# A sketched linear attention feeding an MLP: new order of steps, earlier small loads and table load, attention numerators over four PSUM banks

## The chip, the cores and the metric

The kernel runs on one core of a Trainium2 chip. Its engines each take their instructions in order: TensorE multiplies matrices (in the profile PE, and PEld for the loading of weights), VectorE is DVE, ScalarE is ACT, GpSimd is POOL, and SyncE is SP. SP and ACT also issue DMAs. The metric is the device time of one execution in microseconds (us); lower is better. Engines wait for each other on semaphores.

## The reference

Two parts follow each other. The first is an attention without softmax, for 4 batches, 4 heads, 1088 tokens and 32 values per head. Two sketch matrices S1 and S2 of 8 x 32 turn each query and key into 64 features, the products of 8 values with 8 others:

```python
def phi(x):
    a = np.einsum('rd,bhsd->bhsr', S1, x)
    b = np.einsum('rd,bhsd->bhsr', S2, x)
    return np.einsum('bhsi,bhsj->bhsij', a, b).reshape(*x.shape[:-1], r * r)
q_p, k_p = (phi(q), phi(k))
kv = np.einsum('bhsf,bhsd->bhfd', k_p, v)
z = np.sum(k_p, axis=2)
num = np.einsum('bhsf,bhfd->bhsd', q_p, kv)
den = np.einsum('bhsf,bhf->bhs', q_p, z)[..., None] + 1e-06
return (num / den).astype(np.float32)
```

The second takes the 4352 tokens, each with the 4 heads' 32 values as 128 inputs, through an MLP:

```python
h = x @ w_in                                # 128 -> 2048
g = h * (1.0 / (1.0 + np.exp(-beta * h)))
return (g @ w_out).astype(np.float32)       # 2048 -> 128
```

## The kernel before

**Units.** Each batch's 1088 tokens are laid out as 34 units of 32 tokens and 32 partitions' worth of head values, so that a 32 x 32 block transposition on VectorE (helper `tr`, L161) turns one form into the other. A batch has 9 columns of units in 4 groups (the last group is short).

**Steps and their order.** Nothing is issued as it is written. Every step is registered with `add(engine, name, function, reads, writes)`, and at the end `steps.issue` calls them in the order of the string ORDER (L18), which must respect the reads and writes. So ORDER alone sets the order in which each engine meets its instructions; names in it, such as `kproj1`, `qp2.0.3` or `h4.5`, are the names used below. An element-wise product of any step is the helper `mul` (L152), a copy L156 or L158.

**Set-up.** `fill` and ten `idle` steps give TensorE matmuls of no use to the result (L313). `st` transposes S1 and S2, and `wk`, `wq0`, `wb4` and `wab` lay them out as weights; `s2sel`, `sel`, `rep`, `m4` and `zmask` are selection matrices made from iotas. `beta0` to `beta3` spread beta over the partitions by a matmul of one row (L392), ScalarE copies it out (`betac`), and GpSimd makes `winp` = w_in x beta and `woutp` = w_out / beta in float16 (`w_in`, L407, and `w_out`, L414), so that the activation Silu gives g x beta.

**Keys.** For batch 0, `keys_first` (L491) transposes k in three pieces as its loads arrive, projects it (`kproj0.u`, L509), copies the result to SBUF on ScalarE (`kab`), and forms the 64 features per key on VectorE and GpSimd (`kp`). For batches 1 to 3, `keys` (L537) does the same with block transpositions: `kT`, `kproj` (L546), `kab`, `kp`. In both, `zsum` (`z`, L443) sums features, `wmat` (`W` and its copy `ww`, L460) brings z to the queries' form, `kvsum` (`kv`, L474) makes the features' product with v, and `kvturn` (`kvt`) transposes it. z, W, kv and the later step w all write PSUM bank A2, and each counts as one writer of the whole bank. kv has to stand on all four partition groups: in batch 0 that is a matmul (`km`, then `spread`, L638, and the copy `kvr0`); in batches 1 to 3 it is a DMA to a scratch in DRAM (`scw`, L569) and four DMAs back (`scr`, L575).

**Queries.** The first 8 units of batch 0 go a way of their own (`head`, L590: `abA`, `bS`, `qpA`, `wA`, `numA`, `xA`), so that the MLP can start early. All others go through `queries` (L645): `qproj` (L655) and `w` (L666) on TensorE; `qab`, `qw`, `m`, `den`, `rden`, `an` on VectorE; the 64 features `qp` on VectorE and GpSimd; their transposition `qpT`; and the numerators. These are made in two steps: `numa` for three of the four groups, in the three banks A0, A1, A2 of ATT, a copy `xa` by ScalarE to the float16 array xs, then `numb` for the fourth group in A0 again, and its copy `xb` (L715 for both). Batch 0 has two pieces (`0.8` with 16 units and `0.24` with 10); batches 1 to 3 have one of 34 each.

**The MLP.** `moe` (L767) handles a chunk of up to 16 units, 512 tokens. Its 16 slices of the hidden width go in waves of two (four for the first, short chunk): `h` (L787) puts two products in a pair of PSUM banks W0 or W1, by turns; `s` is Silu by ScalarE over the pair (L793); and two waves later `o` (L800) adds both slices to the bank ACC. After a chunk's last `o`, `acc` transposes the sum into `osb`, and four DMAs store it. Chunks 0 to 2 are batch 0 (8, 16 and 10 units), chunks 3 to 9 the others; the last has 6 units.

**Loads.** SP issues k and q of batch 0 in pieces, then q of batch 1, w_in in two halves, w_out in two halves (rows of 128 values, 512 bytes a run), and the later batches; ScalarE's queue has beta, S1, S2 and the four loads of v. The first Copy and the first Silu on ScalarE are each preceded by a load of its function table.

## Time and profile before

| | |
|---|---|
| device time, median of 3 runs | 127.86 us (127.12 to 130.6) |
| the profiled execution: time | 126.54 us |
| the profiled execution: span, first to last instruction | 124.8 us |
| TensorE busy in the span | 108.9 us, mean granted clock 0.917 |
| ScalarE, VectorE, GpSimd busy | 78.0, 57.1, 43.8 us |
| Silu (76 activations) | 66.9 us |
| first product h, second product o (160 matmuls each) | 43.2 and 38.4 us |

Times are from the span's start unless said otherwise. Slices are fortieths of the span, 3.12 us each. The granted clock is the share of its full speed at which TensorE runs, as the chip's throttle reports it. A row of the timeline gives start, length, engine, line, operation, output and inputs with their shapes, how often, and in brackets the idle time before it and what ended that. fp32 matmuls leave two records each. Busy times of TensorE include the tails of pipelined matmuls, so the distance from one start to the next tells more than the mean length.

### The profile page before, as it was taken

What the parts mean: (1) busy time and instruction counts of PE and PEld (TensorE: products, weight loads), DVE (VectorE), ACT (ScalarE), POOL (GpSimd) and SP (SyncE); (2) the same over time, 40 slices, a digit from 0 to 9 for tenths busy, and PEclk for the clock granted to TensorE, in tenths of its full rate; (3) what the DMA queues carried; (4) which work ended last, traced back from release to release, by engine and by line L of the source; (5) the groups of instructions that cost most, each with busy time, mean ns of one, the idle gap of its engine ahead of it and who ended that gap; (6) DMA issues with size and microseconds to landing.
All of it is one profiled execution on the core that took longest, in us unless ns stands there. A gap on an engine that the chain in (4) does not pass through costs nothing.

```text
span 124.8 us, 3010 instructions
## 1 busy us (share of the span) xinstructions
PE 108.9 (87%) x1240; PEld 55.5 (44%) x1240; DVE 57.1 (46%) x116; ACT 78.0 (62%) x97; POOL 43.8 (35%) x48
## 2 busy tenths in 40 slices
PE   6978799687999999756999998999799999999950
PEld 4667574353563354432244343355243444444550
DVE  3247968990442846792624863032759102011120
ACT  0092101883478957103996996487699899899950
POOL 5025793596400850830490470077065000000000
PEclk9985559965579999999999999999999999999999
DMA  3899999916305302533400101001250210612342
GB/s 86 210 351 299 330 321 248 225 53 220 137 0 123 95 5 59 125 78 53 68 3 16 42 0 21 5 0 26 46 97 18 46 25 7 100 17 32 53 75 41
DMA packets 27404, 11.71 MB, mean 94 GB/s; under 512 B 21100, under 2 KB 26236, under 8 KB 27392
## 3 DMA queue, kind: packets, MB, share of 16 engines
q1 hardware_dynamic: 26312, 10.91, 35.9%
q10 hardware_dynamic: 1080, 0.62, 2.2%
q8 instruction: 9, 0.15, 0.5%
q14 instruction: 3, 0.02, 0.1%
HBM read 9.20 MB, written 2.33 MB: 92 GB/s over the span
## 4 chain that ended last, share of the span: by engine, by line
PE 56%; DVE 16%; DMA 10%; ACT 7%; POOL 4%; issue 3%; ACTq 1%; DVEq 0%; POOLq 0%
PE W L787 17%; PE ACC L800 17%; DMA v_in<-in_v_dram 10%; PE ATT L715 8%; DVE qpT L161 6%; ACT gT L793 4%; POOL qp L152 4%; PE ATT L474 3%; PE ATT L666 2%; DVE qab L161 2%; PE W L474 2%; PE ATT L546 2%; PE ATT L655 1%; DVE qw L161 1%; ACT L793 1%
## 5 line engine op out<-in xcount | busy, mean ns | idle before, releaser
L793 ACT ACTIVATE gT<-W 128x1024 f16<-128x1024 f32 (+2 forms) x76 | 66.9, 938 | 11.2 <-PE W L787 10.5
L787 PE MATMUL W<-xs,winp 128*128 128x512 f16 (+3 forms) x160 | 43.2, 362 | 2.7 <-ACT gT L793 2.3
L800 PE MATMUL ACC<-gT,woutp 128*128 128x512 f16 (+3 forms) x160 | 38.4, 356 | 0.8 <-DVE osb L161 0.8
L152 POOL TENSOR_TENSOR kp<-kab 128x512 f32<-128x512 f32 (+2 forms) x11 | 16.6, 1534 | 24.6 <-DVE kab L161 14.5
L787 PEld LDWEIGHTS <-winp 128*128 128x128 f16 x160 | 14.1, 101 | 22.1 <-issue 13.1
L800 PEld LDWEIGHTS <-woutp 128*128 128x128 f16 x160 | 15.9, 102 | 15.9 <-issue 3.2
L152 POOL TENSOR_TENSOR qp<-an,qab 128x768 f32<-128x768 f32 (+1 forms) x8 | 14.3, 1806 | 21.1 <-DVE an L152 17.7
L161 DVE STREAM_TRANSPOSE osb<-ACC 128x512 f32<-128x512 f32 (+3 forms) x10 | 6.2, 623 | 24.0 <-PE ACC L800 24.0
L715 PE MATMUL ATT<-qpT,kvr 32*32 32x288 f32 (+4 forms) x320 | 10.9, 368 | 2.9 <-DVE qpT L161 1.9
L156 ACT CAST xs<-ATT 128x864 f16<-128x864 f32 (+5 forms) x10 | 5.0, 502 | 13.3 <-PE ATT L715 11.3
L161 DVE STREAM_TRANSPOSE qpT<-qp 128x768 f32<-128x768 f32 (+1 forms) x13 | 11.2, 894 | 4.6 <-POOL qp L152 4.5
L715 PEld LDWEIGHTS ATT<-qpT,kvr 32*32 32x32 f32 x320 | 5.7, 112 | 8.2 <-DVE qpT L161 3.3
L161 DVE STREAM_TRANSPOSE kab<-ATT 128x288 f32<-128x288 f32 x6 | 2.6, 469 | 10.7 <-PE ATT L546 10.7
L161 DVE STREAM_TRANSPOSE qT<-q_in 128x1088 f32<-128x1088 f32 (+2 forms) x5 | 5.3, 1050 | 0.1
L156 ACT ACT_TABLE_LOAD x1 | 1.3, 1283 | 6.3 <-DMA v_in<-in_v_dram 6.3
L313 PE MATMUL ATT<-fill 128*128 128x256 f16 x20 | 4.3, 413 | 1.1 <-DVE fill L307 1.1
L152 POOL TENSOR_TENSOR winp<-w_in_sb,beta_bc 128x512 f16<-128x512 f32 x4 | 5.2, 1317 | 0.0
L161 DVE STREAM_TRANSPOSE qab<-ATT 128x288 f32<-128x288 f32 (+2 forms) x10 | 3.7, 386 | 2.8 <-PE ATT L474 2.0
L509 PE MATMUL ATT<-wk,kp 128*128 128x64 f32 x18 | 3.5, 347 | 1.1 <-ACT kab L156 0.6
L161 DVE STREAM_TRANSPOSE qw<-ATT 128x288 f32<-128x288 f32 (+2 forms) x5 | 2.0, 407 | 4.8 <-PE ATT L666 2.4
L666 PE MATMUL ATT<-qT,ww 128*32 128x288 f32 (+2 forms) x40 | 3.1, 381 | 1.3 <-DVE qab L161 0.8
L152 POOL TENSOR_TENSOR woutp<-w_out_sb,rb 128x512 f16<-128x512 f32 x4 | 4.0, 1046 | 0.0
(91 smaller groups left out, 82.8 us busy)
## 6 DMA issues: line engine op xcount, KB each, us to landing
q_in<-in_q_dram SPq DMA_DIRECT2D x3, 544.0 KB, 5.7
k_in<-in_k_dram SPq DMA_DIRECT2D x3, 544.0 KB, 5.9
v_in<-in_v_dram SPq DMA_DIRECT2D x9, 144.0 KB, 4.3
out_dram<-osb SPq DMA_DIRECT2D x20, 64.0 KB, 2.0
w_in_sb<-in_moe_w_in_dram SPq DMA_DIRECT2D x2, 512.0 KB, 7.4
w_out_sb<-in_moe_w_out_dram SPq DMA_DIRECT2D x2, 512.0 KB, 9.0
v_in<-in_v_dram ACTq DMA_DIRECT2D x3, 144.0 KB, 3.4
q_in<-in_q_dram SPq DMA_DIRECT2D x1, 416.0 KB, 5.3
```

Of the source, the lines that this page charges most:

```text
L152: ENG[eng].tensor_tensor(out=o, in0=i0, in1=i1, op=op)
L156: nc.scalar.copy(out=o, in_=i)
L161: nc.vector.transpose(out=o, in_=i)
L313: mm(out=bk("A2", 0, [[1, 256]]), lhsT=f16fill[:, 0:P], rhs=f16fill, start=True, stop=True)
L474: mm(out=bk(bank, 128, [[1, F]], T * h, T), lhsT=v_in[i2][:, h, u, :], rhs=kp[i2][:, u, h, :], start=u == 0, stop=u == KU - 1,)
L509: lambda u=u, c0=c0, bank=bank: mm(out=bk(bank, (u - c0) * 64, [[1, 64]]), lhsT=ap(kp[KTF], u * P, [[1, P]]), rhs=wk.rearrange("p h r -> p ...
L546: mm(out=ATT[T * g : T * g + T, rp, 0 : KU * T], lhsT=wab[64 * rp : 64 * rp + 64].rearrange("p a b -> p (a b)"), rhs=ap(kT, KU * g * T, [[ ...
L666: mm(out=ATT[T * g : T * g + T, 2, 0:nt], lhsT=ap(ww[i2], 0, [[1, H * R]]), rhs=ap(qT[i2], (u0 + n * g) * T, [[1, nt]]), start=True, stop= ...
L715: mm(out=ATT[T * h : T * h + T, bank(g), 0 : gn * T], lhsT=ap(kvr[i2], fb * ft + h * ht, [[1, D]], p0=T * g, pn=T), rhs=ap(qpT[pi], h * F ...
L787: mm(out=place(jj), lhsT=winp[:, j * P : j * P + P], rhs=xs[:, x0 : x0 + n], start=True, stop=True)
L793: nc.scalar.activation(out=g[:, js[0] : js[0] + per, 0:n], in_=src, func=ACTF.Silu)
L800: mm(out=ACC[:, 0:n], lhsT=woutp[:, j, :], rhs=g[:, j, 0:n], start=j == 0, stop=j == NJ - 1)
```

## The change

**Order and engines.** ORDER is another string, and a second string, CHOICE, sets for about 80 steps which of two engines runs them (letters D, G, A for VectorE, GpSimd, ScalarE); it takes the place of the fixed engines.

**Loads and table.** k of batch 0 is one load of whole rows, q of batch 0 is in three pieces, with the first 8 units ahead of k. v of batch 0 moves from ScalarE's queue to SP, the second copy of S2 and the second form of beta move to ScalarE's queue. w_in and w_out come in quarters. w_out is read in runs of four rows per partition (2 KB), so hidden value 4p + j of a quarter now belongs to slice j, and the product `winp` reads w_in and beta four elements apart to match. A Silu of one column (`silu`) is issued at the start, ahead of all copies. The idle steps are 30, each two matmuls of 224 columns, in columns of A1 that nothing else uses; ORDER has six at the start, six up to the fourth wave of chunk 0, and the others in and after chunks 8 and 9.

**Beta.** The four rows are one step, placed after `kproj0` and before `z0`.

**Banks.** z and W get columns 288 to 352 of A0 and keys of their own; kv keeps A2. kp is in pieces, and kv is made piece by piece. The keys of batch 0 are copied in five pieces, and VectorE's kp reads one input from PSUM.

**Numerators.** `numa` and `numb` become one step over four banks: A0, A1 and one pair of W, which counts as a wave in the turns of W0 and W1. Two copies, `xa` and `xb`, take two groups each; in batches 1 to 3 VectorE makes `xa` and ScalarE `xb`.

**Batch 1** uses `km`, `spread` and `kvr1` as batch 0 does, and no scratch; batches 2 and 3 keep it.

**Chunks.** The numerators of a batch are placed between waves of a chunk; chunk 8's and 9's waves are interleaved, and chunk 9 sums in A0.

```diff
@@ ORDER, its start, the stretch up to batch 1's numerators, batch 2's scratch, the end
+fill idle0 epsA iop eps1 dma.q0a wq0z qTz1 zAz kTfz dma.k0 idle1 idle2 idle3 vcol id16 hcol tcol1 tcol0 tsel8
+ones dma.q0b sel dma.s1 dma.q0c mask1 dma.v0.2 idle4 mask0 dma.s2 qT0.0 st idle5 dma.s3 tsel128 wk dma.v0.3
+wq0 s2sel abA rep wb4 kTz eps0 qTz0 bS vz1 dma.v0.1 kT0.2 silu kproj0.3 kproj0.4 dma.v0.0 dma.b16 abAt dma.b4
+kT0.0 kproj0.2 vz0 kab0.3 dma.win1 kT0.5 kT0.6 kproj0.1 wab kproj0.0 kab0.1 dma.win3 qT0.8 qpA kproj0.5 bSc
+kproj0.6 kp0.3 kab0.0 kp0.0 kp0.1 kproj0.8 kab0.5 qT0.24 kproj0.7 kab0.7 dma.win2 beta z0 kv0.0 kv0.1 kv0.3
+kp0.5 betac1 kp0.7 kp0.8 qpAt ztm0 zA dma.win0 winp1 kv0.5 kv0.7 kv0.8 betac3 betac0 qproj0.8 kvt0 km0 wA
+spread0 s2bd winp3 W0 qab0.8.1 qab0.8.0 qproj0.24 dma.wout1 wAt dma.wout2 mA kvr0 idle6 ww0 qab0.24.0 dma.q1
+w0.8 betac2 winp0 numA denA rdenA qw0.8 rdT w0.24 betaT idle7 m0.8 xA h0.0 den0.8 qab0.24.1 rden0.8 winp2 s0.0
+dma.wout0 qw0.24 dma.k1 an0.8 dma.k2 idle8 h0.1 m0.24 qp0.8.2 den0.24 idle9 qp0.8.0 qpT0.8.2 rden0.24 an0.24
+h0.2 idle10 idle11 s0.1 s0.2 rb qpT0.8.0 kT1 h0.3 s0.3 dma.wout3 woutp0 dma.v2.0 num0.8 woutp1 xa0.8 xb0.8
+o0.0 woutp2 kproj1 dma.v1.0 qp0.24.2 dma.v1.2 qT1.0 h1.0 dma.v1.1 dma.v2.3 kab1.0 kab1.1 s1.0 h1.1 dma.v2.2
+o0.1 z1 dma.v1.3 kp1.0 ztm1 h1.2 s1.1 W1 qp0.24.0 qproj1.0 h1.3 ww1 dma.v2.1 woutp3 w1.0 qpT0.24.0 kp1.2 s1.2
+h1.4 dma.q2 s1.3 s1.4 qab1.0.0 qpT0.24.2 o0.2 kp1.4 h1.5 o0.3 s1.5 qw1.0 kv1.0 qab1.0.1 m1.0 num0.24 acc0
+den1.0 xa0.24 kv1.2 h1.6 kv1.4 kp1.6 xb0.24 s1.6 h1.7 kv1.6 dma.k3 o1.0 h2.0 s1.7 s2.0 rden1.0 an1.0 o1.1 h2.1
+s2.1 o1.2 qp1.0.3 dma.st0.2.0 kvt1 qp1.0.0 dma.st0.1.0 h2.2 dma.q3 km1 o1.3 qp1.0.6 dma.st0.0.0 s2.2 qpT1.0.0
+h2.3 s2.3 qpT1.0.3 spread1 h2.4 kvr1 dma.v3.0 qpT1.0.6 o1.4 s2.4 o1.5 num1.0 h2.5 kT2 o1.6 o1.7 dma.v3.2 xb1.0
...
+o2.6 o2.7 acc2 kv2.0 dma.st2.3.24 rden2.0 an2.0 h3.7 kv2.2 s3.7 kv2.4 kv2.6 h3.6 h4.1 o3.0 kvt2 s3.6 s4.1 o3.1
+o3.2 h4.0 dma.scw2 o3.3 kT3 s4.0 qp2.0.6 qpT2.0.6 dma.st2.1.24 qp2.0.3 h4.3 qp2.0.0 s4.3 o3.4 h4.2 o3.5 o3.6
+qpT2.0.0 s4.2 qpT2.0.3 dma.scr2.0 dma.scr2.3 dma.scr2.1 h4.4 dma.scr2.2 s4.4 o3.7 num2.0 acc3 o4.0 xb2.0 h4.6
...
+idle13 o9.7 dma.st8.1.114 idle14 idle15 idle16 idle17 idle18 idle19 idle20 acc9 dma.st9.0.130 dma.st9.2.130
+dma.st9.3.130 dma.st9.1.130 idle21 idle22 idle23 idle24 idle25 idle26 idle27 idle28 idle29
@@ loads
-    load_v("ACT", 0)
+    load_cols("SP", k, k_in[0], "k0", 0, 0, U * D, ["k0.a", "k0.b", "k0.c"])
     load_cols("SP", q, q_in[0], "q0a", 0, 0, HEAD * D, ["q0.a"])
+    load_v("SP", 0)
...
+                out=w_out_sb[:, 4 * i : 4 * i + 4, :].rearrange("p j m -> p (j m)"),
+                in_=moe_w_out[512 * i : 512 * i + 512, :].rearrange("(p j) m -> p (j m)", p=P),
@@ idle and the table load
-            mm(out=bk("A2", 0, [[1, 256]]), lhsT=f16fill[:, 0:P], rhs=f16fill, start=True, stop=True)
+            mm(out=bk("A1", 288, [[1, 224]]), lhsT=f16fill[:, 0:P], rhs=f16fill[:, 0:224], start=True, stop=True)
+    add(
+        "ACT", "silu", lambda: nc.scalar.activation(out=warm, in_=f16fill[:, 0:1], func=ACTF.Silu),
+        r=["fill"], w=["warm"],
+    )
@@ w_in
-            eng, f"winp{i}", lambda: mul(eng, winp[:, c], w_in_sb[:, c], beta_bc[:, c]),
+            eng, f"winp{i}", lambda e: mul(
+                e, ap(winp, 512 * i, [[P, 4], [1, P]]), ap(w_in_sb, 512 * i, [[1, 4], [4, P]]),
+                ap(beta_bc, 512 * i, [[1, 4], [4, P]]),
+            ),
@@ zsum, wmat
-                    out=ATT[T * c : T * c + T, 2, 0:32], lhsT=ap(kab[i2], u * 64 + 1, [[2, H * R]]),
+                    out=ATT[T * c : T * c + T, 0, 288:320], lhsT=ap(kab[i2], u * 64 + 1, [[2, H * R]]),
...
-                out=ATT[:, 2, 64:96], lhsT=s2bd.rearrange("p h d -> p (h d)"),
+                out=ATT[:, 0, 320:352], lhsT=s2bd.rearrange("p h d -> p (h d)"),
@@ keys_end (new)
+        if b == 1:
+            add(
+                "D", "km1",
+                lambda e: mul(e, km, ap(kvt[1], 0, [[T, 2], [0, H], [1, T]]), ap(m4, 0, [[0, 2], [1, H], [0, T]])),
+                r=["kvt1", "m4"], w=["km"], alts="DG",
+            )
+            spread(1)
+            return
@@ betas (new)
+        def beta_rows():
+            for i, b_ in enumerate(banks):
+                mm(out=BANK[b_], lhsT=ones[T * i : T * i + 1, :], rhs=b4[T * i : T * i + 1, :], start=True, stop=True)
+
+        add("PE", "beta", beta_rows, r=["b4", "ones"], w=banks)
@@ queries_end
+            banks = [ATT[:, 0], ATT[:, 1], W[i][:, 0], W[i][:, 1]]
...
+                for fb in range(2):
+                    for h in range(H):
+                        for g in range(4):
+                            mm(
+                                out=banks[g][T * h : T * h + T, 0:nt],
+                                lhsT=ap(kvr[i2], fb * ft + h * ht, [[1, D]], p0=T * g, pn=T),
+                                rhs=ap(qpT[pi], (po * H + h) * F + fb * T, [[H * F, n], [1, T]], p0=T * g, pn=T),
+                                start=fb == 0, stop=fb == 1,
+                            )
@@ the main sequence
+    end1 = batch(1)
+    moe(HEAD, 16, 2, {6: n024})
+    n1 = end1()
+    moe(HEAD + 16, 10, 2, {SLOT[1]: n1})
     moe(34, 16, 2)
-    moe(50, 16, 2)
-    batch(3)
+    n2 = batch(2)()
+    moe(50, 16, 2, {SLOT[2]: n2})
     moe(66, 16, 2)
-    moe(82, 16, 2)
+    n3 = batch(3)()
+    moe(82, 16, 2, {SLOT[3]: n3})
     moe(98, 16, 2)
-    moe(114, 16, 2)
-    moe(130, 6, 2)
+    c8, c9 = Chunk(114, 16), Chunk(130, 6, 2, "A0")
+    for c in LAST:
+        (c8 if c == "8" else c9).wave()
```

More of the change, by code (lines that the diff above doesn't have):

```diff
@@ L740 @@
+        return num
     pend = []
@@ L810, in moe @@
             pend.append(second)
             flush(2)
+    def moe(s0, sn, per=2, between={}):
+        ch = Chunk(s0, sn, per)
+        for w in range(NJ // per):
+            if w in between:
+                between[w]()
+            ch.wave()
     def cut(*engs):
```

487 lines of the change are left out of this document (265 added, 222 removed).

## The prediction

> **What bounds the kernel now.** I read the page's forty slices and its chain of waits first, then a table of stretches cut where the granted clock changes.
>
> ```profile
> span 124.8 us, 3010 instructions
> PE   6978799687999999756999998999799999999950
> PEclk9985559965579999999999999999999999999999
> PE 56%; DVE 16%; DMA 10%; ACT 7%; POOL 4%; issue 3%; ACTq 1%; DVEq 0%; POOLq 0%
> ```
>
> TensorE carries more than half of the chain, so what counts is when it is idle and when it runs slowly. The slices show three such places: the head (granted clock 0.5 in slices 3 to 5), slices 8 to 11 (0.5 again), and slices 17 to 19 (full clock, TensorE idle).
>
> ```profile
> 8.50:11.90 3.40, 2.31 (x11) 0.51 1.04 302
> 15.35:18.76 3.41, 3.41 (x83) 0.50 1.11 316
> 18.76:22.20 3.44, 3.24 (x32) 1.00 1.03 247
> ...
> 22.25:25.60 3.35, 1.80 (x14) 1.32 (x14) 3.13 (x8) 3.22 (x4) 2.48 (x3) 1.00 0.93 208
> 25.60:35.84 10.24, 9.54 (x112) 4.87 (x111) 4.96 (x10) 5.55 (x8) 5.94 (x6) 0.50 0.33 116
> 50.00:62.40 12.40, 9.22 (x142) 3.98 (x140) 8.26 (x11) 4.34 (x7) 5.04 (x3) 1.00 0.42 80
> 99.00:112.00 13.00, 13.00 (x73) 5.59 (x71) 0.75 (x2) 12.18 (x14) 0.00 (x0) 1.00 0.26 40
> ```
>
> The columns are the stretch, its length, TensorE's busy time (the last four rows add weight load, VectorE, ScalarE and GpSimd), clock, DMA share and GB/s. A full stretch of 3.41 at 15.35 is followed by full clock; one with 1.80 busy of 3.35 at 22.25 is followed by 10.24 us at half clock. Only from 35.84 on does the array run at full speed to the end, and there 50.0 to 62.4 is the one stretch with over 3 us of idle TensorE. At 99 to 112 TensorE (13.00) and ScalarE (12.18 in 14 activations, so about 0.93 each) are both full: nothing can be won there.
>
> **The head, to the first matmul of the MoE part (T).** Now T is 22.25, and a table load stands between it and the first activation.
>
> ```profile
> 3.94 0.84 DVE L161 STREAM_TRANSPOSE kp<-k_in 128x640 f32<-128x640 f32 x1 [1.28 <-DMA k_in<-in_k_dram]
> 5.31 1.33 PE L392 MATMUL W<-b,ones 1*128 1x512 f32 x6
> 7.29 1.33 PE L509 MATMUL ATT<-wk,kp 128*128 128x64 f32 x10
> 9.11 1.12 PE L509 MATMUL ATT<-wk,kp 128*128 128x64 f32 x4 [0.49 <-DVE kp L161]
> 11.71 1.17 PE L597 MATMUL W<-qT,wq 128*128 128x256 f32 x2
> 12.67 1.06 PE L602 MATMUL W<-qT,wb 128*128 128x256 f32 x2
> 14.83 2.15 PE L474 MATMUL W<-kp,v_in 128*32 128x64 f32 x72 [0.64 <-DMA v_in<-in_v_dram]
> 17.04 0.25 DVE L161 STREAM_TRANSPOSE kvt<-W 128x64 f32<-128x64 f32 x1 [1.19 <-PE W L474]
> 17.32 1.18 DVE L152 TENSOR_TENSOR km<-kvt,m 128x256 f32<-128x256 f32 x1
> 21.12 0.42 DVE L152 TENSOR_TENSOR xs<-W,rdT 128x256 f16<-128x256 f32 x1
> 22.25 1.34 PE L787 MATMUL W<-xs,winp 128*128 128x256 f16 x8
> 22.95 1.28 ACT L793 ACT_TABLE_LOAD   x1
> ```
>
> The v load, now moved ahead of all weights, held the kv product back by 0.64 only, so its earlier landing alone is worth no more. What decides is TensorE's own chain, which the change reorders: S first, then abA and bS, nine kproj, all four beta rows in one step, z, kv. The first loads land by 3.94, so with the three S loads first on ScalarE's queue I put st at 4.3, wk at about 4.9 and abA at 5.3, against 11.71. From there, counted by these rows: abA and bS 2.1; a kproj is two records, 0.27 at full clock (10 records in 1.33) and 0.55 at half (4 in 1.12), so nine are 2.4 or 5.0; about 0.6 of waiting for ScalarE's copies between them; beta is eight records of 0.22, so 1.8 or 3.6; z about 0.35 or 0.5; kv 1.2 or 2.15 (half clock as shown, full clock by halving, an estimate). Begun at 5.3, this ends at 13.75 with full clock after bS, at 19.25 with half clock throughout. Now beta stands beside waiting for loads; here it is on the path, which is the price of moving it. After kv comes VectorE's run to xA: 17.04 to 21.54 now, 4.5; qpAt leaves it and four short steps of the next piece enter, so 5.0. T is then 18.75 at best and 24.25 at worst. TensorE is busy without a real gap from 5.3, and a full 3.4 us of that was followed by full clock at 18.76, so I take release at about 12: T = 21.0. Loads do not enter: v's four issues move from ScalarE's queue to SP behind k and q, and all of v and of w_in go out ahead of w_out and q1. The table load goes to the time before data arrive, where it costs nothing.
>
> The new w_in product reads both inputs four elements apart, where now they lie side by side. No row shows this; the nearest are
>
> ```profile
> L152 POOL TENSOR_TENSOR winp<-w_in_sb,beta_bc 128x512 f16<-128x512 f32 x4 | 5.2, 1317 | 0.0
> L152 POOL TENSOR_TENSOR qp<-an,qab 128x768 f32<-128x768 f32 (+1 forms) x8 | 14.3, 1806 | 21.1 <-DVE an L152 17.7
> ```
>
> so 1.32 to 1.81 each, and I take 1.32. GpSimd makes three of them and the third is needed only some 1.5 us after T, so the sum holds at both ends. [...]
>
> **From T to batch 1's num.** Now num1 starts 33.1 us after T:
>
> ```profile
> 21.46 0.30 DVE L161 STREAM_TRANSPOSE qw<-ATT 128x128 f32<-128x128 f32 x1
> ...
> 24.74 0.71 DVE L161 STREAM_TRANSPOSE qpT<-qp 128x512 f32<-128x512 f32 x1
> 25.38 1.27 DVE L161 STREAM_TRANSPOSE qT<-q_in 128x1088 f32<-128x1088 f32 x1
> 39.99 0.93 DVE L161 STREAM_TRANSPOSE kab<-ATT 128x288 f32<-128x288 f32 x2 [2.45 <-PE ATT L546]
> 41.06 4.43 POOL L152 TENSOR_TENSOR kp<-kab 128x1024 f32<-128x1024 f32 x3 [6.61 <-DVE kab L161]
> 47.02 0.69 PE L666 MATMUL ATT<-qT,ww 128*32 128x288 f32 x8 [0.36 <-DVE qab L161]
> 47.78 0.48 DVE L161 STREAM_TRANSPOSE qw<-ATT 128x288 f32<-128x288 f32 x1 [0.81 <-PE ATT L666]
> ...
> 49.73 0.46 DVE L152 TENSOR_TENSOR an<-qab,rden 128x288 f32<-128x288 f32 x1
> 52.59 2.69 DVE L161 STREAM_TRANSPOSE qpT<-qp 128x768 f32<-128x768 f32 x3
> 55.33 1.47 PE L715 MATMUL ATT<-qpT,kvr 32*32 32x288 f32 x48 [1.40 <-DVE qpT L161]
> 57.77 0.96 PE L715 MATMUL ATT<-qpT,kvr 32*32 32x224 f32 x16 [0.97 <-ACT xs L156]
> L152 DVE TENSOR_TENSOR qp<-an,qab 128x768 f32<-128x768 f32 x3 | 3.1, 1038 | 0.1
> ```
>
> Two things made it late. Batch 1 starts (kproj1, kab at 39.99) only behind chunk 0, half of chunk 1 and both pieces of batch 0; and z, W, kv and w share bank A2, so that w (47.02) stands behind GpSimd's kp (41.06 to 45.49) and kv. With z and W in columns of A0, w needs only z, and with kproj1 placed right after the first o step the chain is VectorE's own. From T: the nine steps between 21.46 and 25.45 (3.8 busy) less the first two, which now come before T, plus five of the second piece at about 0.26, so 4.5; kT1 and qT1 at 1.27; kab at T + 7.0. From kab: kab 0.93, four steps of 512 elements at 0.71 (kp, qp, qpT and woutp3, by the qpT row) 2.8, two of 256 at 0.42 0.85, two qab 0.93, five steps qw to an 2.4 (47.78 to 50.19), two qp at 1.04, ztm and kvt 0.45, km1 1.18, three qpT 2.69: 14.3. km1 and the spread product replace the scratch round trip for this batch, and lie in this sum. I add 1.0 for the clock: the stretch after T has TensorE perhaps three quarters busy, between the 1.80 of 3.35 that lost the clock and the 3.24 of 3.44 that kept it, and the idle matmuls between the first waves are there to fill it. [...] So num1 = 21.0 + 7.0 + 14.3 + 1.0 = 43.3, against 55.33.
>
> **The rest.** TensorE does less by then:
>
> ```profile
> 51.60 2.33 PE L800 MATMUL ACC<-gT,woutp 128*128 128x320 f16 x16 [0.81 <-DVE osb L161]
> 119.54 1.15 PE L800 MATMUL ACC<-gT,woutp 128*128 128x192 f16 x12
> ```
>
> Left behind num1 are all of chunk 2's second products (2.33), six of its first (6 of 0.146, 0.9) and four of chunk 1 (0.43 a pair, the pitch of chain rows after 99, 0.86): 4.1. The rest takes 120.69 - 55.33 = 65.4 now. Num over four banks is 64 records in one step. If four row groups run side by side as three do now it stays at 1.47; if records pass at the present rate (48 in 1.47) it is 1.96; I take 1.7, for 1.47 + 0.96, three times: 2.1 less. The wait for xs between the two halves (0.97 in batch 1) goes. The wave takes a pair of W banks, so one activation waits behind it; the copies are split over two engines for that, and I count nothing (from 1 us less to 3 us more, since the stretch without attention, where ScalarE's 0.93 a wave is the bound, grows by half a chunk). The idle matmuls after the last product run beside the last store. So the last product ends at 43.3 + 65.4 + 4.1 - 2.1 - 1.0 = 109.7, against 120.69. The same 4.1 behind it gives a span of 113.8; the execution profiled took 126.54 for 124.8, so 115.6, and the median shown is 1.3 above that execution: **117.0**.
>
> **Rivals.** (a) The clock is not held: no release before T (T = 24.25) and one more stay of 10.24 us at half clock behind it. The row at 25.60 shows that 9.54 busy of 10.24 does not release it when the work is small tiles; the idle matmuls speak against. Price 3.25 for T and 4 for the stay (half of 10.24 less the 1.0 already counted), so 124.2. Chance 0.15. (b) The same, with VectorE slowed beside a busier GpSimd (km took 1.18 where xs of the same 256 elements took 0.42) or the tail bound by ScalarE: 2 to 4 more, 125.5 to 129, no change. Chance 0.08. (c) Slower: the in-order SP queue. In batches 2 and 3 the scratch loads still stand in it behind stores.
>
> ```profile
> SPq L753 <- DVE osb L161: 39.6, 9, 8.9
> ```
>
> A store waited up to 8.9 us for its transpose. If that comes ahead of both scratch loads, num2 and num3 are held, and behind them in TensorE's order every h and o: 117.0 + 2 x 8.9 = 134.8, or more than 130.4 once each waits over 6.7. Against it: the stores placed ahead are of chunks whose transposes come before kvt on VectorE. Chance 0.05. (d) Better than counted (clock released at 8.5, num at 1.47): 111 or so, 0.07. The forecast case has 0.65.
>
> **The numbers.** The range takes the bounds of T (2 down, 3 up), clock, num and tail, without all falling on one side: 112 to 123.5. It leaves out (b), (c), part of (a) and of (d). Two per cent, about what a measurement can tell here, is 2.6 us: faster below 125.3 is the forecast, (a) and (d), 0.87; within 0.08; slower 0.05.
>
> **What would show it.** The first activation table load before 5 us; first MoE matmul between 19 and 24; no half clock after it; num1 at 41 to 46 with TensorE waiting under 2 us for it; winp's mean on GpSimd; num steps of 1.5 to 2.0; the last second product near 110. Half clock past 25, or a num waiting for scratch loads, would make the prediction wrong.

## The result

The changed kernel takes 130.58 us (median of 4 runs, 130.38 to 131.18), the kernel before 127.49 beside it (4 runs, 126.73 to 130.6). The ratio is 1.028, with a 95% interval from 1.022 to 1.034; it leaves out the run of 130.6 of the kernel before, which is a slow one. That is slower by 3%, where 117.0 was forecast. The execution profiled took 130.38 us for a span of 128.6. The first lines of its page, with the granted clock and the shares of the chain by engine:

```profile
span 128.6 us, 3119 instructions
PE   6497495759999977999959999979999998989985
PEclk9999999999999999999999999999999999999999
PE 62%; ACT 17%; DVE 11%; DMA 4%; issue 3%; SPq 1%; ACTq 1%; DVEq 0%
```

The line of the clock has to be read with care. The trace holds only the changes of the grant, and the page puts full clock where it has seen none yet. In this execution the first change on record is a release (the step from half to full clock) at 37.1 us; the rows before it run at half rate (four records of a key projection take 1.12, the price of half clock in the kernel before, and the first wave 1.06, where later ones of its size take 0.60). So the whole head ran at half clock.

Three distances hold the result. T is the start of the first MoE matmul; the tail goes from the end of the last second product to the end of the span.

| | T | from T to the last second product | tail | span |
|---|---|---|---|---|
| before | 22.25 | 98.44 | 4.11 | 124.8 |
| forecast | 21.0 | 88.7 | 4.1 | 113.8 |
| after | 34.42 | 89.04 | 5.14 | 128.6 |

The body gave 9.4 us of the 9.7 that the forecast took from it. The head lost 12.2, the tail 1.0. The head by stretches (TensorE's busy time is the second figure), then its timeline:

```profile
8.50:16.10 7.60, 4.98 (x23) 4.11 (x21) 3.49 (x8) 1.28 (x5) 2.80 (x3) 1.00 0.90 302
16.10:22.30 6.20, 4.68 (x106) 2.79 (x114) 2.50 (x5) 1.83 (x4) 4.00 (x4) 1.00 0.63 254
22.30:34.40 12.10, 9.65 (x70) 6.02 (x70) 6.03 (x16) 1.05 (x3) 4.20 (x2) 1.00 0.53 139
```

```profile
6.61 1.22 PE L676 MATMUL W<-qT,wq 128*128 128x256 f32 x2
10.21 1.12 PE L552 MATMUL ATT<-wk,kp 128*128 128x64 f32 x4 [0.35 <-ACT kab L183]
14.36 0.69 PE L552 MATMUL ATT<-wk,kp 128*128 128x64 f32 x2 [1.56 <-DVE kp L179]
16.03 2.09 PE L642 MATMUL W<-b,ones 1*128 1x512 f32 x8
18.39 1.25 PE L509 MATMUL ATT<-kp,v_in 128*32 128x64 f32 x37
19.30 5.09 POOL L179 TENSOR_TENSOR winp<-w_in_sb,beta_bc 128x512 f16<-128x512 f32 x2 [2.20 <-ACT beta_bc L183]
19.80 0.43 DVE L179 TENSOR_TENSOR kp<-ATT,kab 128x256 f32<-128x256 f32 x1 [5.08 <-ACT beta_bc L183]
21.17 1.08 PE L509 MATMUL ATT<-kp,v_in 128*32 128x64 f32 x32 [1.52 <-DVE zA L179]
23.25 1.43 DVE L179 TENSOR_TENSOR km<-kvt,m 128x256 f32<-128x256 f32 x1
29.25 2.11 POOL L179 TENSOR_TENSOR winp<-w_in_sb,beta_bc 128x512 f16<-128x512 f32 x1 [4.85 <-ACT beta_bc L183]
30.34 1.17 DVE L179 TENSOR_TENSOR prod<-qab,qw 128x128 f32<-128x128 f32 x1
31.75 0.42 DVE L179 TENSOR_TENSOR xs<-W,rdT 128x256 f16<-128x256 f32 x1 [0.24 <-PE W L709]
32.12 2.03 PE L653 MATMUL ACC<-id,beta 4*128 4x4 f32 x8
34.42 1.06 PE L891 MATMUL W<-xs,winp 128*128 128x256 f16 x4
```

The forecast had TensorE "busy without a real gap from 5.3". Between 8.5 and 16.1 it works 4.98 of 7.60. A key projection waits for ScalarE's copy of the piece before (0.35 each), one for VectorE's kp (1.56), and the last kp piece comes only at 19.80. km and prod, small steps on VectorE, take 1.43 and 1.17 where a product of as many elements or more, xs, takes 0.42; each ends just behind a strided piece of winp on GpSimd (24.68 behind 24.39, and 31.51 behind 31.36). betaT's 2.03 stand between xA and the first wave.

Behind T the steps came as forecast, 22.4 after it instead of 22.3 (batch 1's numerators at 56.78, the first row), and the last second product 66.7 behind these instead of 66.4. The other rows are the tail:

```profile
56.78 0.43 PE L824 MATMUL ATT<-qpT,kvr 32*32 32x288 f32 x2
...
123.14 0.32 PE L908 MATMUL ATT<-gT,woutp 128*128 128x192 f16 x2
123.30 1.50 PE L350 MATMUL ATT<-fill 128*128 128x224 f16 x14
124.84 0.38 DVE L188 STREAM_TRANSPOSE osb<-ATT 128x192 f32<-128x192 f32 x1 [2.72 <-DMA out_dram<-osb]
125.26 0.87 ACTq L858 DMA_DIRECT2D out_dram<-osb  x2
```

The last transposition starts 1.4 us behind the last product. By the profile a store released it: chunk 9 uses the buffer of chunk 6, one of whose stores stands late in SP's queue.

### The profile page after: what moved, and what is told of

Its sections match the earlier page's. It is cut to its first block, busy times and chain, and to the rows that moved or that the text cites. A ratio compares the mean times of both kernels' runs of the same rounds, so it can differ in the third digit from the quotient of the medians.

```text
span 128.6 us, 3119 instructions
## 1 busy us (share of the span) xinstructions
PE 112.9 (88%) x1288; PEld 61.4 (48%) x1288; DVE 63.6 (49%) x126; ACT 75.6 (59%) x100; POOL 41.6 (32%) x49
## 4 chain that ended last, share of the span: by engine, by line
PE 62%; ACT 17%; DVE 11%; DMA 4%; issue 3%; SPq 1%; ACTq 1%; DVEq 0%
PE W L891 15%; ACT gT L901 15%; PE ACC L908 15%; PE ATT L509 5%; PE ATT L552 4%; PE ATT L824 4%; PE ATT L350 4%; DMA s_in<-in_S_dram 3%; DVE qab L188 2%; PE ATT L752 2%; PE W L824 2%; PE ATT L741 2%; PE ATT L587 2%; PE W L642 2%; PE W L709 2%
## 5 line engine op out<-in xcount | busy, mean ns | idle before, releaser
L901 ACT ACTIVATE gT<-W 128x1024 f16<-128x1024 f32 (+2 forms) x76 | 66.7, 947 | 18.7 <-PE W L891 18.1
L908 PE MATMUL ACC<-gT,woutp 128*128 128x512 f16 (+2 forms) x144 | 36.5, 359 | 0.0
L179 POOL TENSOR_TENSOR kp<-kab 128x512 f32<-128x512 f32 (+2 forms) x14 | 16.8, 1223 | 22.4 <-DVE kab L188 18.4
L891 PEld LDWEIGHTS <-winp 128*128 128x128 f16 x160 | 14.8, 102 | 19.1 <-issue 8.7
L188 DVE STREAM_TRANSPOSE osb<-ACC 128x512 f32<-128x512 f32 (+2 forms) x9 | 6.0, 664 | 22.5 <-PE ACC L908 22.4
L179 POOL TENSOR_TENSOR qp<-an,qab 128x768 f32<-128x768 f32 (+2 forms) x6 | 9.1, 1524 | 12.4 <-DVE an L179 12.4
L188 DVE STREAM_TRANSPOSE qpT<-qp 128x768 f32<-128x768 f32 (+2 forms) x14 | 11.3, 836 | 0.0
L350 PE MATMUL ATT<-fill 128*128 128x224 f16 x60 | 9.5, 302 | 2.1 <-DVE fill L345 1.1
L179 POOL TENSOR_TENSOR winp<-w_in_sb,beta_bc 128x512 f16<-128x512 f32 x3 | 7.2, 2415 | 7.1 <-ACT beta_bc L183 7.1
L509 PE MATMUL ATT<-kp,v_in 128*32 128x64 f32 x288 | 7.1, 245 | 2.1 <-DVE zA L179 1.5
L350 PEld LDWEIGHTS <-fill 128*128 128x128 f16 x60 | 6.2, 109 | 3.3 <-issue 1.4
L824 PE MATMUL ATT<-qpT,kvr 32*32 32x288 f32 (+2 forms) x160 | 7.0, 353 | 0.7 <-DVE qab L188 0.6
L179 DVE TENSOR_TENSOR qp<-an,qab 128x768 f32<-128x768 f32 (+1 forms) x7 | 7.5, 1076 | 0.0
L824 PE MATMUL W<-qpT,kvr 32*32 32x288 f32 (+2 forms) x160 | 6.7, 354 | 0.0
```

The source lines that it names most:

```text
L179: ENG[eng].tensor_tensor(out=o, in0=i0, in1=i1, op=op)
L188: nc.vector.transpose(out=o, in_=i)
L350: mm(out=bk("A1", 288, [[1, 224]]), lhsT=f16fill[:, 0:P], rhs=f16fill[:, 0:224], start=True, stop=True)
L509: mm(out=ATT[T * h : T * h + T, 2, 128 : 128 + F], lhsT=v_in[i2][:, h, u, :], rhs=kp[i2][:, u, h, :], start=u == 0, stop=u == KU - 1,)
L824: mm(out=banks[g][T * h : T * h + T, 0:nt], lhsT=ap(kvr[i2], fb * ft + h * ht, [[1, D]], p0=T * g, pn=T), rhs=ap(qpT[pi], (po * H + h) * F ...
L891: mm(out=W[i][:, half, rest * n : rest * n + n], lhsT=winp[:, j * P : j * P + P], rhs=xs[:, x0 : x0 + n], start=True, stop=True,)
```

## The experiments

Three theories of the head. **A**: it is late because the array runs at half clock. **B**: it is late because the new order puts waits on other engines and small products in series with TensorE. **C**: the strided read of the w_in product slows GpSimd, and VectorE beside it. A and B are told apart by T, since A asks for a large fall once the clock is full. All runs are in one table. Each kernel ran once but for e9 (five runs) and e10 (four), where the time is the median; the other columns are of the execution profiled. The changed kernel, e1 and e7 have nearly the same head, and their T (34.42, 34.76, 34.55) shows how much of a difference is noise.

| | T | T to the last second product | tail | time |
|---|---|---|---|---|
| e1 more idle work at the start | 34.76 | 89.03 | 5.21 | 130.74 |
| e2 key projections back to back | 32.11 | 89.76 | 5.13 | 128.80 |
| e3 w_in read as it lies | 33.45 | 89.04 | 5.21 | 129.44 |
| e4 betaT behind the second wave | 32.00 | 91.07 | 5.13 | 130.04 |
| e5 idle work in all waits | 39.23 | 89.30 | 5.67 | 136.07 |
| e6 head in another order | 27.03 | 88.76 | 5.11 | 122.72 |
| e7 tail | 34.55 | 89.43 | 4.02 | 129.79 |
| e8 before, half the idle work | 21.22 | 98.31 | 4.07 | 125.40 |
| e9 e6 and e7 together | 25.32 | 88.79 | 4.19 | 121.49 |
| e10 e9 with beta early | 27.30 | 88.58 | 4.22 | 121.87 |
| e11 e6 with the strided read | 29.54 | 89.02 | 5.14 | 125.45 |
| e12 kp read from SBUF | 32.62 | 90.07 | 5.11 | 129.58 |

### The clock: e1, e5, e8

e1, 20 idle matmuls ahead of the first data instead of 10:

```diff
-    def idle():
-        for _ in range(2):
+    def idle(n):
+        for _ in range(n):
...
+    IDLES = {0: 4, 1: 4, 2: 4, 3: 4, 4: 4}
```

> The changed kernel with 20 idle matmuls instead of 10 ahead of the first data (four in each of the first five idle steps), so that TensorE is busy from 1.06 us to about 4.9 without a gap; nothing else differs. Changed kernel: first MoE matmul (T) at 34.42, last second product ends 123.46, the profiled execution took 130.38. Theory A (the head is late because the array runs at half clock until 37): the clock is released by 5 to 8.5, the nine key projections take 0.27 each where they do not wait, and T falls by 4 to 7, to 27.5 to 30.5; the time is 124 to 127. Theory B (the head is late because of waits that the new order puts in series: copies between the projections, kp readers of the same bank, beta rows on the path): the clock may be released, but T falls by less than 2 (33 or later), and the time is 129 to 131. Theory C (the strided w_in product): no change.

T stayed, at 34.76, but the run doesn't decide: the trace has no release before the first wave, although TensorE was busy without a gap from 1.06 to 4.97. So e5 put idle steps into every wait of the head (the new ones in the order, the counts in IDLES):

```diff
-kproj0.2 ... kproj0.1 ... kproj0.5 ... kproj0.8 ... kproj0.7 ...
+kproj0.2 ... idle30 kproj0.1 ... idle31 kproj0.5 ... idle32 kproj0.8 ... idle33 kproj0.7 ...
```

> The changed kernel with idle matmuls put into every wait that its trace shows in the head: 20 ahead of the first data, 14 behind S's product, and 3 to 12 in the waits between the key projections, before beta, z, the second half of kv, the spread product and the query products (110 in all in place of 16 there); order and all real work as in the changed kernel. The 20 at the start alone left T at 34.76. Theory A (half clock makes the head late, and the earlier run only missed a whole window of dense work): a release shows before 10 us, and T falls by 4 or more, to 30 or less; time 126 or less. Theory B (waits in series; the rate of the array hides behind other engines): even with full clock in part of the head T stays within 1.5 of 34.4, time 129 to 132.

Now the release came, at 5.5, and held to 12.3 us (a record of the trace). In the traces the distance from one change to the next is a multiple of 3.41 us (10.2, 6.8 and 10.2 in the kernel before, from 8.5 to 35.8; 6.8 and 17.1 here, from 5.5 to 29.4), and such a step is called a window below; this release held for two. Timeline and stretches of e5:

```profile
9.97 0.57 PE L555 MATMUL ATT<-wk,kp 128*128 128x64 f32 x4
11.18 0.57 PE L555 MATMUL ATT<-wk,kp 128*128 128x64 f32 x4
13.30 2.40 PE L351 MATMUL ATT<-fill 128*128 128x224 f16 x12 [1.55 <-DVE kp L180]
```

```profile
5.50:12.30 6.80, 5.54 (x42) 4.74 (x43) 3.27 (x10) 0.81 (x3) 3.59 (x9) 1.00 0.88 233
12.30:29.40 17.10, 13.97 (x156) 9.29 (x156) 4.82 (x10) 2.31 (x6) 5.90 (x4) 0.50 0.43 168
```

Groups of projections take 0.57 instead of 1.12, and yet the wait for kp stands there as before, 1.55. From the start of abA to the end of the third group it takes 4.2 instead of 6.2 (7.58 to 11.75, and 6.61 to 12.81), so two windows of full clock gained 2.0 us; half of that was lost ahead of abA, where S came 0.5 later and more idle steps stand. T rose to 39.23, which neither theory asked for, since at half clock the idle steps themselves came onto the path (2.40 for twelve); that part of the rise says nothing on A. From 29.4 on the clock was full again, and the stretch from the end of kv to the end of xA took 8.8 (28.34 to 37.09) instead of 9.9; but there too idle steps stand on the path (0.93, 0.73 and 0.64), so this doesn't price the clock. e8 asked the same of the kernel before:

```diff
     def idle(i):
-        for _ in range(2):
+        for _ in range(1):
```

> The kernel before with half of its idle matmuls (10 of 20 ahead of the first data), so that no whole window is dense by 5.1 us; nothing else differs. If the release at 5.1 to 8.5 and again at 18.8 is what makes the earlier kernel's head short (theory A): the first MoE matmul, 22.25 before, comes at 24 to 26 and the time rises by 2 to 4 over the profiled 126.5. If it is its order (theory B): T stays within 1 of 22.25, and the time within 1.5.

With its projections now at half clock (14 records in 3.25) the earlier kernel reached T at 21.22, an us sooner than with the early release. T moved by 1.0, and not the way that A asked (24 to 26), so an early release is not what makes its head short. What it had in both executions is full clock behind kv, from 15.5 here and from 18.8 in the kernel before; the run says nothing on how much that is worth.

### The order and the stride: e2, e12, e3, e4

e2 issues the nine projections in a row and lets VectorE's kp read the copy in SBUF; e12 does only the latter.

```diff
-            kprod(0, eng, o0, on, [f"kab0.{c0}"], place(o0))
+            kprod(0, eng, o0, on, [f"kab0.{c0}"])
...
+kproj0.3 kproj0.4 kT0.0 kproj0.2 kproj0.1 kproj0.0 kT0.5 kT0.6 kproj0.5 kproj0.6 kproj0.7 kproj0.8 bSc kab0.3 kab0.1 kab0.0 kab0.5 kab0.7
```

> The changed kernel with all nine key projections of batch 0 issued back to back ahead of ScalarE's five copies (and bS's copy ahead of these), and with kp read by VectorE from the copy in SBUF, as in the kernel before, and not from the PSUM bank. Idle matmuls and all else as in the changed kernel. Theory A (half clock alone): the projections take 5.0 in a row at half clock, no less than that, and T falls by 2.5 or less; the clock stays at half to about 35. Theory B (waits in series): projections end near 13.5 instead of 16.1, kp's last piece no longer waits until 19.8, kv ends near 19 instead of 22.25, and T falls by 3 to 4, to 30.5 to 31.5; time 126.5 to 128. Theory C (strided w_in product on GpSimd sets the start of the first wave): T stays above 33, because the first product still starts behind its beta copy at 29.25.

> The changed kernel with kp's three VectorE pieces of batch 0 read from the copy in SBUF instead of the PSUM bank, and no change of order. If it is the reader in the bank that holds the key projections and the last kp piece (waits of 1.56 ahead of one projection and of 5.08 ahead of kp's last piece): both waits shrink (under 0.6; kp's last piece starts before 17.5), kv ends by 20.5 instead of 22.25 and T falls by 1 to 2. If the copies piece by piece are the cause: T within 0.6 of 34.42.

In e2 the projections are one run of 3.94 and T is 32.11; in e12, with the reads alone, it is 32.62. The last kp piece and the second half of kv in e12:

```profile
14.68 0.42 DVE L179 TENSOR_TENSOR kp<-kab 128x256 f32<-128x256 f32 x1 [1.24 <-ACT kab L183]
18.42 1.08 PE L509 MATMUL ATT<-kp,v_in 128*32 128x64 f32 x32 [0.53 <-DVE zA L179]
```

Five us earlier than 19.80, and the 1.56 ahead of one projection is 0.30. So the new PSUM read, a part of the change that the forecast gave no price, held both TensorE and VectorE. By the times, the last kp piece had stood behind kv's first half (ended 19.64, start of kp 19.80), although the two touch different banks of that PSUM tile. The profile of the changed kernel names a copy of beta that ended at 19.71 instead; in e5, where the copies end at 22.34 and kv's first half at 23.50, it names kv for the piece that starts at 23.66. Why the one waits for the other is not shown. In e12 kv ends 2.75 earlier (19.50), but T gains only 1.8: km then started earlier inside a GpSimd piece and took 2.06. So it did in e2, which gained less than B asked (30.5 to 31.5).

e3 reads w_in and beta side by side again, with w_out's rows and betaT to match; the diff shows the product:

```diff
-                e, ap(winp, 512 * i, [[P, 4], [1, P]]), ap(w_in_sb, 512 * i, [[1, 4], [4, P]]),
-                ap(beta_bc, 512 * i, [[1, 4], [4, P]]),
+                e, winp[:, c], w_in_sb[:, c], beta_bc[:, c],
```

> The changed kernel with the w_in product read as it lies in memory again (blocks of 128 columns side by side, w_out rows loaded to match, beta turned to match); order, engines and all else as in the changed kernel. Theory C (reading four elements apart is what slows GpSimd and, beside it, VectorE): GpSimd's winp falls from 2415 ns to 1320 each, km from 1.43 to about 1.2, prod from 1.17 to about 0.3, and T by 1 to 2, to 32.5 to 33.5; time 128 to 129.5. Theory A or B: winp falls as said, but T by less than 0.8, and the time stays at 129.5 to 131.

T fell by 0.97, just short of what C asked (1 to 2), where A and B asked for under 0.8. winp on GpSimd took 1271 ns instead of 2415, km 0.42, since GpSimd's two pieces had ended (22.00) before it began (23.44), and prod 0.33.

e4:

```diff
-w0.8 ... w0.24 betaT idle7 m0.8 xA h0.0 ... idle8 h0.1 ...
+w0.8 ... w0.24 m0.8 xA h0.0 ... idle8 h0.1 betaT ...
```

> The changed kernel with the four small products that turn beta (2.03 us, 8 records) placed behind the second MoE wave instead of ahead of the first, and without the idle step between them and the first wave; nothing else differs. If they lie on the path (theory B): T falls from 34.42 to about 32.3, where xA (32.17) and the first w_in product (31.36) hold it, and the time by 1.5 to 2.2, to 128 to 129. If what counts is that the clock is released only after a full busy stretch (theory A): without them TensorE has a gap there, the release at 37.2 comes later by a window of 3.4 us, and the time stays within 1 of 130.4.

```profile
32.00 0.77 PE L893 MATMUL W<-xs,winp 128*128 128x256 f16 x4
...
32.87 0.60 PE L893 MATMUL W<-xs,winp 128*128 128x256 f16 x4
33.39 2.02 PE L655 MATMUL ACC<-id,beta 4*128 4x4 f32 x8
...
36.90 1.06 PE L893 MATMUL W<-xs,winp 128*128 128x256 f16 x4
```

Each theory is half right. T fell by 2.4, as B asked, but the time only by 0.3 against the profiled execution, as A asked: the 2.0 were paid behind T. betaT takes 2.02 here, at full clock (32.4 to 35.8), as it took 2.03 at half clock in the changed kernel, and after it the waves are back at 1.06. The trace shows half clock from 35.8 to 39.2.

### The head in another order: e6 and e11

e6 adds to e2: the contiguous read, all w_in pieces on GpSimd, the third beta copy with the others, betaT in four parts, each in a wait, and no idle steps 6 and 7.

```diff
-spread0 s2bd winp3 W0 qab0.8.1 qab0.8.0 qproj0.24 ... w0.8 betac2 winp0 numA ... w0.24 betaT idle7 m0.8 xA h0.0
+spread0 s2bd W0 qab0.8.1 qab0.8.0 betaT0 qproj0.24 ... betaT1 w0.8 betaT2 numA ... betaT3 w0.24 m0.8 xA h0.0
```

> The changed kernel with its head put in another order and nothing done about the clock: nine key projections back to back and kp read from SBUF (these two alone gave T = 32.11); w_in product read as it lies (alone T = 33.45) and all four pieces on GpSimd, none on VectorE ahead of km; the third beta copy with the others; z's two products ahead of the last kp piece's followers; the four small beta products one each in waits of 0.5 to 0.65 that stand in TensorE's order anyway, and no idle step before the first wave. Theory B with C (waits and shared-memory contention): km back to 1.2 to 1.4, T at 27 to 29.5, last second product at T + 89, time 123 to 125.5. Theory A (half clock is what costs): T no lower than 31, time above 127.

The second half of kv and xA in e6:

```profile
16.69 1.08 PE L510 MATMUL ATT<-kp,v_in 128*32 128x64 f32 x32 [0.50 <-DVE zA L179]
...
26.14 0.42 DVE L179 TENSOR_TENSOR xs<-W,rdT 128x256 f16<-128x256 f32 x1 [1.67 <-PE W L711]
```

T is 27.03, at the early end of what B with C asked, and the time 122.72, a little below it. Nothing was done about the clock: the trace has no change on record, and the rows of the head run at half rate (the nine projections 3.94 as in e2, the first wave 1.01). Of the 7.4 that T gained, abA, bS and the key projections gave 3.7 (9.5 to 5.8), z and kv 1.0 (4.1 to 3.1), the stretch from kv to xA 1.1 (9.9 to 8.8) and that from xA to the first wave 1.8 (2.3 to 0.5); abA began 0.2 later. How this divides among e6's edits only the single ones tell (T 2.3 earlier in e2, 1.0 in e3, 2.4 in e4). e11 then puts only the strided read back into e6, with w_out's rows and betaT to match:

```diff
-                e, winp[:, c], w_in_sb[:, c], beta_bc[:, c],
+                e, ap(winp, 512 * i, [[P, 4], [1, P]]), ap(w_in_sb, 512 * i, [[1, 4], [4, P]]),
+                ap(beta_bc, 512 * i, [[1, 4], [4, P]]),
```

> The reordered head (T = 27.03, where the four w_in pieces took 1.31 each on GpSimd and km 0.49, prod 0.25) with only the strided read of the w_in product put back. Theory C as the traces now suggest it (a VectorE operation with two inputs in SBUF that starts beside a GpSimd instruction ends 0.15 to 0.3 after that instruction does, so a longer GpSimd instruction costs VectorE as well): winp 2.4 to 2.55 each, running from 16.5 to about 26.5; km or prod, whichever starts inside a piece, ends 0.15 to 0.3 behind that piece's end; T later by 1.5 to 3.5, at 28.5 to 30.5. If GpSimd's work only runs beside (rival): km and prod stay under 0.6, and T within 0.5 of 27.0.

GpSimd's second piece and km, first in the timeline of e6, then of e11:

```profile
17.73 1.26 POOL L179 TENSOR_TENSOR winp<-w_in_sb,beta_bc 128x512 f16<-128x512 f32 x1
...
18.78 0.49 DVE L179 TENSOR_TENSOR km<-kvt,m 128x256 f32<-128x256 f32 x1
```

```profile
16.49 4.21 POOL L179 TENSOR_TENSOR winp<-w_in_sb,beta_bc 128x512 f16<-128x512 f32 x2
...
18.61 2.37 DVE L179 TENSOR_TENSOR km<-kvt,m 128x256 f32<-128x256 f32 x1
...
23.21 1.90 DVE L179 TENSOR_TENSOR prodA<-abA,wA 128x64 f32<-128x64 f32 x1
```

In e6 the piece ends at 18.99 and km at 19.27; in e11 the second piece ends at 20.70 and km at 20.98. Both times 0.28 later, whether the piece took 1.26 or some 2.1: as if km waited until GpSimd's instruction was over and did its work then. So a longer piece can cost it more: km took 2.37 here, 0.49 in e6. prodA meets GpSimd's last piece, which ends at 25.03, and takes 1.90 instead of 0.23 in e6. A piece took 2168 ns, less than the 2400 expected, but T came 2.51 later for this one edit, within what C asked (28.5 to 30.5), so C holds, through VectorE more than through GpSimd. The clock doesn't explain it: e11 had full clock from 17.9 to 21.3, where e6 had none.

### The tail: e7

```diff
+    def osb_of(c):
+        return w_in_sb[:, 0:512].rearrange("p (u m) -> p u m", u=16) if c == 9 else osb[c % NO]
...
-                tr(osb[c % NO][:, 0 : self.sn, :].rearrange("p u m -> p (u m)"), bk(self.acc, 0, [[1, n]])),
+                tr(osb_of(c)[:, 0 : self.sn, :].rearrange("p u m -> p (u m)"), bk(self.acc, 0, [[1, n]])),
```

> The changed kernel with the last chunk's output transposed into memory of its own (w_in's tile, unused by then) instead of the buffer whose earlier stores stand late in SP's queue, and without the 16 idle steps behind the last second product; nothing else differs. If the tail's extra 1.0 (5.14 from the last second product to the end of the span, where the kernel before took 4.11) comes from that buffer: the transpose follows the last product within 0.3 instead of 1.4, the tail is 3.9 to 4.2, and the time 129 to 129.5. If the last stores or SP's order set the end: the tail stays above 4.8.

```profile
123.65 0.33 PE L912 MATMUL ATT<-gT,woutp 128*128 128x192 f16 x2
124.02 0.38 DVE L187 STREAM_TRANSPOSE w_in_sb<-ATT 128x192 f32<-128x192 f32 x1 [1.38 <-PE ATT L912]
```

The transposition follows at once and the tail is 4.02, 1.1 shorter. Against the profiled execution of the changed kernel (130.38) the time fell by 0.6 only, since the head and body of this one were 0.5 longer. The idle steps went in the same run, so their part is not told apart.

### A version that beats both: e9 and e10

e9 is e6 with e7's edit. 

> The reordered head (alone: first MoE matmul at T = 27.03, last second product at T + 88.8, tail 5.1) together with the last chunk's own output memory and no idle steps behind the last product (alone: tail 4.02). If head and tail are independent terms of one sum, as theory B has it: T 27.0, tail 4.0 to 4.1, span 119.8 to 120.0, time 121.4 to 122.0, against 127.5 of the kernel before: a ratio near 0.954. If part of the head's gain is given back later: above 123.

121.49 us (median of 5, 120.11 to 121.82), the kernel before beside it 127.06 (7 runs, 124.58 to 129.36): the slowest run of e9 is 2.8 below the fastest of the kernel before. The two edits add up. The execution profiled was the fastest of the five; there a release at 19.4 held for one window, to 22.8, and from the end of kv (17.28) to T it took 8.0, where e6 at half clock took 9.3 (17.77 to 27.03). By these two executions a window of full clock is worth some 1.2 us there, an estimate. The other 0.5 of the earlier T lie ahead of kv's end.

e10 moves beta's rows into the wait for the first data and betaT into the wait for kp, and lets VectorE's kp read PSUM again, now ahead of z and kv:

```diff
-"ACT", "b4",
+"SP", "b4",
...
+... qT0.0 beta0 beta1 st beta2 beta3 ... silu betac0 betac1 betac2 betac3 abA ... kproj0.8 ... kp0.7 betaT z0 ...
```

> The kernel of the run before with the head changed once more: beta's four row products run while TensorE waits for the first data (its load first on SP's queue), the four small beta products stand where TensorE waits for kp, kp's three VectorE pieces read the PSUM bank again but all stand ahead of z and kv, S2's selection is made early, and one w_in piece runs on GpSimd ahead of kp. By the rows of the reordered head: kv ends near 17.2 instead of 17.8, and behind it TensorE has 1.2 for the spread, 1.2 for wA, 0.7 and 0.6 for the query products, 0.5 for W, 2.1 for numA and 1.2 for w, some 7.5 with its waits, so T = 24.5 to 26 (theory B), time 119 to 120.7. If the half clock behind kv is what is left (theory A): T stays at 26.5 or more, time above 121.

A miss: T 27.30, and 121.87 us (4 runs), the outcome that A asked for. Its timeline shows waits too that took time back:

```profile
9.39 0.27 ACTq L304 DMA_DIRECT2D beta<-in_moe_beta_dram  x1
13.77 1.83 PE L656 MATMUL ACC<-id,beta 4*128 4x4 f32 x8 [0.58 <-DMA beta<-in_moe_beta_dram]
...
18.78 0.25 DVE L187 STREAM_TRANSPOSE kvt<-ATT 128x64 f32<-128x64 f32 x1 [2.27 <-PE ATT L744]
19.07 1.29 DVE L178 TENSOR_TENSOR km<-kvt,m 128x256 f32<-128x256 f32 x1
```

beta's second load, behind the beta copies on ScalarE's queue, went out at 9.39 instead of 2.11 and betaT waited for it; the transposition of kv waited for the query product issued ahead of it (0.68), and km met a GpSimd piece again. kv ended at 18.07 instead of the 17.2 expected, and from there to T it took 9.2 at half clock instead of 7.5. What the half clock and what the waits took of this is not told apart.

## Why the prediction was wrong

**What failed is the step that put T at 21.0, and at 24.25 at worst.** It counted TensorE's own records at both clocks, with 0.6 of waiting, on the ground that TensorE is "busy without a real gap from 5.3". Both bounds varied the clock; the waits on other engines, which the new order put in series with TensorE, had no price, and neither had betaT. e6, with many of these waits out and no release before T, has T 7.4 earlier. Against the forecast's case with half clock throughout (24.25) the 10.2 missing us are, from the timeline of the changed kernel:

- 1.3 ahead of abA (6.61 instead of 5.3): S came at 4.90 instead of 4.3, and S2's product and an idle step stood between.
- 1.8 in the key projections (from 8.68 to 16.1, 7.4 instead of 5.6): the copies and the PSUM reads. In a row the nine take 3.94 at half clock (e2), not the 5.0 of the forecast, so the waits here are 3.5, not 0.6. Removing the reads alone gave T 1.8, with the projections in a row 2.3 (e12, e2).
- 1.6 less for beta (2.0 instead of 3.6): its records come 0.25 apart at half clock, not twice 0.22.
- 1.5 in z and kv (4.1 instead of 2.65): the last kp piece, late for the same reason.
- 4.9 from kv to xA (9.9 instead of 5.0). The forecast took the earlier kernel's run of VectorE, which had full clock behind kv, and added names to it. Here it ran at half clock, with a w_in piece on VectorE, km and prod behind GpSimd's strided pieces, and the second query piece's products in TensorE's way. How much each of these is worth stays open: in e6, without the stride and the w_in piece, 8.8 are left at half clock.
- 2.3 for betaT and an idle step ahead of the first wave. The forecast priced "all four beta rows in one step" and left betaT out; e4 shows that it cost its length, ahead of the first wave and behind it. The forecast had nothing at all between xA and the first wave, where the kernel before has 0.7 (21.54 to 22.25).

**The clock.** "Release at about 12" did not come; the first is at 37.1. The forecast drew it from one row, a stretch of 3.41 fully busy that was followed by full clock. Counted back from 37.08 in windows of 3.41, and taking them to run on evenly, TensorE was busy for a whole window from 6.36 to 9.77 and again from 30.25 to 33.67, each time without a release; in e9 it was for two in a row, from 5.77 to 12.60. The release of e9 at 19.4 came behind a window with 3.22 of 3.41 busy, in 51 records of TensorE, and that of e11 at 17.9 behind one with 2.92, in 102; the full window from 6.36 had 12. So a busy TensorE does not by itself bring the release, and what does is not shown. No release before T is the condition of rival (a), whose price was T = 24.25 and 124.2 us. By e5 and e9, an estimate, a window at full clock is worth 1.0 to 1.2 us in the head; this is no part of the 10.2, which stand against half clock throughout. How far T would fall in e9 with full clock through the head was not tried.

**winp** was taken at 1.32, the contiguous row, with a slack on GpSimd that should hide it. It took 2.415. No row of before had a read four elements apart; the measured factor is 1.66 between e6 and e11 (1308 and 2168 ns), 1.83 in the changed kernel, where VectorE makes a piece of its own beside it. But the slack on GpSimd was the wrong thing to check: the cost came through VectorE (e11). The row km, 1.18, was seen, and used as a rival of 2 to 4 us with a chance of 0.08.

**The body came out right**: T to num1 22.4 (forecast 22.3, with the 1.0 for the clock), the rest 66.7 (66.4), no wait for scratch loads (TensorE idles 0.7 in all ahead of the num steps, for other things), a num step of 1.6 (1.7). VectorE's chain set num1, as forecast: its last qpT ends at 56.64, num1 starts at 56.78. That the sum agrees to 0.1 is in part luck, since inside it errors cancel: woutp3 and one qp took 1.55 and 1.36 instead of 0.71 each and two waits 0.55 and 0.84, while km1 took 0.41 instead of 1.18. Every run that kept the body shows 88.6 to 91.1 from T to the last product, so an us in the head was nearly an us in the end, but for e4, which moved work across T. e2, e7 and e12 have 0.7, 0.4 and 1.0 more than the changed kernel there. Their release came 3.8, 4.2 and 4.7 us behind T instead of 2.7, so more of their waves ran at half clock; that this is the reason fits, but no run varied it alone.

**The tail** was carried over as 4.1 on the ground that idle matmuls run beside the store; the buffer shared with chunk 6 was not looked at. The last transposition waited 1.4 for it, and the tail is 1.1 shorter without it and the idle steps (e7).

**The rivals.** The kernel is slower, but not by rival (c): no scratch load was late. The conditions of (a), no release before T, and of (b), VectorE slowed beside GpSimd, both came, and their prices were too small. (b) is also given wider, 125.5 to 129, than 2 to 4 on top of 124.2 make it.

## What to carry to other kernels

Before summing one engine's records along a reordered stretch, list for each of its instructions which other engine has to finish first, and give each such wait a price; a sum of busy times with two clocks was no bound here (24.25 at worst, and T came at 34.42). When a product is moved or strided on GpSimd, look at what VectorE does beside it (km 2.37 instead of 0.49 in e11), not only at whether GpSimd is in time. Compare kernels by distances between the same events (first wave, last product, end): here two of three were off by 0.3 and 1.0 us, and the third held 13.4 of the 14.8 us by which the span was off.

## What the hardware showed that was not expected

- Three operations of VectorE with two inputs in SBUF ended a little behind the GpSimd piece that was running when they started: km 0.28 us in e6 (18.99 and 19.27), e11 (20.70 and 20.98) and e2 (22.08 and 22.36), prod with half of the elements 0.15 in the changed kernel (31.36 and 31.51), prodA with a quarter 0.08 in e11 (25.03 and 25.11). That is as if their work began only then; the traces do not show why. It did not happen to all: a qp on VectorE that started 0.01 behind one on GpSimd (27.99 and 27.98, e6) took 0.68, while GpSimd's took 1.63. A transpose and an operation with one input from PSUM kept their usual length beside w_in pieces (qpAt 0.70 in the changed kernel, s2bd 0.28 in e6). With strided pieces it went the other way too: with VectorE's own w_in piece between them, two pieces on GpSimd took 5.09 in the changed kernel, where e11 has two in 4.21. With contiguous ones it did not (two in 2.50 in e3, VectorE's piece between them; four in 5.12 in e6, without one).
- Nearly four us of dense idle matmuls do not always release the clock. 3.91 from 1.06 on did not (e1), 4.33 from 1.05 on did (the kernel before, at 5.1), 3.91 from 1.06 on did in e5 (at 5.5), and the kernel before with half of them got its first release on record at 15.5 (e8). So the same start can go both ways; that it depends on where the windows fall in an execution is a guess. The seven runs of the kernel before go from 124.58 to 129.36, the fastest with the highest mean clock (0.927) and the slowest with the lowest (0.885), so the clock may be what spreads them. e10's four runs lie within 0.13, though their mean clocks differ (0.96 to 1.00).
